# Decode attention plus SwiGLU on one core: the 38-row transfer of the output weights cut into 26 and 12 rows, and two strips of x moved from SyncE's DMA queue to GpSimd's

## The chip, the cores and the metric

The kernel runs on one core of a Trainium2 chip. A core has TensorE (PE; its weight loads are PEld), VectorE (DVE), ScalarE (ACT), GpSimd (POOL) and SyncE (SP), each with its own instruction queue, and 16 DMA engines. The metric is the device time of one execution in microseconds (us); lower is better. A profiled execution also gives a span, from the first to the last instruction of the core.

## The reference, cut to what matters

A transformer block for one new token in each of B = 4 sequences, with D = 640 channels, 32 heads of Dh = 192, and a window of W = 2048 cached positions; all in bf16.

```
xn  = layernorm(x)
q   = xn @ wq                                    # 640 x 6144
p   = softmax(q . k_cache[:, :, -2048:, :] * 192**-0.5)
o   = p . v_cache[:, :, -2048:, :]
a   = o @ wo                                     # 6144 x 640
f   = (silu(xn @ w1) * (xn @ w3)) @ w2           # 640 x 1536, 1536 x 640
out = x + a + f
```

Nearly all the bytes are read once: 201 MB of keys and values, 7.9 MB each of wq and wo, 3.9 MB of w1 and w3, 2.0 MB of w2.

## The kernel before, in words

**Layout.** A tile of keys or values holds 128 partitions (32 heads x 4 blocks of positions), each with 128 positions x 192 channels: 6144 KB, one transfer by `load` (issue at L109). The pool `kv` has three such buffers, so a load waits on SP until the tile that used its buffer three loads earlier has been read. A sequence needs four loads of keys and four of values.

**Keys** (`keys`): VectorE multiplies a quarter of the tile by the broadcast q (L211), TensorE adds 16-channel pieces by matmuls against an identity (L218), VectorE reduces the rest (L228). **Softmax** (`chain`): maximum, exponent (L251), row sums (`rowsum`). **Values** (`values`): VectorE spreads the probabilities over the heads (z, L267), and 64 matmuls (L279) multiply them by the tile; `evict` (L287) and `sort` (L295, L297) bring the result of a sequence into `oT`, the left operand of the output projection.

**Order.** The lists `units` and `stream` write out the order by hand: loads run ahead of their use by two. The last entries of `stream` are `gates` (w1 and w3 into one kv buffer, L320), `last_values` (the last tile of values as two halves, VS = 2, and then WI = 10 of the NI = 48 rows of the output weights that each partition holds, into a buffer of the pool `pr`), and `last_weights` (the other 38 rows of the output weights into a kv buffer, L304, and then w2 in three pieces of 8, 3 and 1 rows, L325). All of these are issued from SP, one behind another, on one DMA queue (q1 in the profile). `dve` and `pe` pin the order of the instructions of VectorE and TensorE to that of the program.

**End of the kernel.** `ffn_mm` (L332) and `ffn_transpose` (L348) make the gated hidden vector while the last values come in. Then the two halves of the last values, `evict`, `sort`, and `proj` (L311): for each of the 48 rows of the output weights two matmuls of 320 columns, first the 10 rows, then the 38 rows (76 matmuls). `acc` collects them. VectorE copies `acc` (L411) and adds `x_st` (L412). TensorE runs 24 matmuls of w2 (L419, two for each of its 12 rows), VectorE adds both (L422), and SP and ACT store half of the output each (L424, L425).

**The strips of x.** `x_st` holds x once more, cut in two strips of 320 columns at partitions 0 to 3 and 32 to 35, so that it has the layout of `acc`. GpSimd clears the tile (L120). `x_load` fills it by two DMAs of 2.5 KB from SP (L124); it is called in the main loop when the keys of sequence 2 begin.

Of the kernel before, what the change touches and what calls it, by code (L numbers as in the profile page):

```python
# [18 lines left out]
def kernel(  # L19
# [13 lines left out]
    CH: int = 32,  # L33
    R: int = 4,
    WI: int = 10,
    ALIGN: int = 64,
):

# [6 lines left out]
    nc = tc.nc  # L45
    P = 128
    B, Sq, D = A_x.shape
    _, H, Sk, Dh = A_k_cache.shape
# [3 lines left out]
    NJ = P  # L52
# [5 lines left out]
    NI = Dh // R  # L58
# [4 lines left out]
    DH = D // 2  # L63
# [12 lines left out]
    kvpool = ctx.enter_context(tc.tile_pool(name="kv", bufs=3))  # L76
    ppool = ctx.enter_context(tc.tile_pool(name="pr", bufs=2))
# [25 lines left out]
    def load(which, b, s, n0=0, n1=NJ):  # L103
        if n0 == 0:
            kv = kvpool.tile([P, NJ, Dh], BF16, tag="kv")
            kvs[which, b, s] = kv
        p0 = Sk - W + s * NJ * R
        rows = {"k": A_k_cache, "v": A_v_cache}[which][b, :, p0:p0 + NJ * R, :].rearrange("h (r n) d -> h r n d", r=R)
        nc.sync.dma_start(out=kvs[which, b, s][:, n0:n1, :].rearrange("p n d -> p (n d)"),  # L109
                          in_=rows[:, :, n0:n1, :].rearrange("h r n d -> h r (n d)"))  # L110
# [6 lines left out]
    x_rows = A_x.rearrange("b s d -> (b s) d")  # L117
    nc.scalar.dma_start(out=x_bf[:, 0, :], in_=x_rows)
    x_st = const.tile([64, DH], BF16, name="x_st")
    nc.gpsimd.memset(x_st[:], 0.0)  # L120

    def x_load():
        for t in range(2):
            nc.sync.dma_start(out=x_st[32 * t:32 * t + B, :], in_=x_rows[:, t * DH:(t + 1) * DH])  # L124

    wq_rows = A_wq.rearrange("(p kc) n -> p kc n", kc=KC)
    wq0 = kvpool.tile([P, NJ, Dh], BF16, tag="kv")
# [26 lines left out]
    at = (NH - 1) * NG * R  # L154
    for b in range(B):
        nc.vector.tensor_copy(out=qwin[:, b, at:at + NG * R].rearrange("p (g r) -> p g r", r=R),
                              in_=idf[:, b:P:32].unsqueeze(2).to_broadcast([P, NG, R]))
# [29 lines left out]
    for k in range(NH // 2):  # L187
        pool, tag = (ps_add, "ps") if k < 2 else (ps_o, "o_ps")
# [109 lines left out]

    wos, ffn = {}, {}

    def wo_load(i0, i1, pool, tag, shape):
        wt = pool.tile(shape, BF16, tag=tag)
        flat = wt[:].rearrange("p a n -> p (a n)")[:, 0:(i1 - i0) * D]
        nc.sync.dma_start(out=flat, in_=A_wo.rearrange("(p i) n -> p i n", i=NI)[:, i0:i1, :].rearrange("p i n -> p (i n)"))  # L304
        for i in range(i0, i1):
            wos[i] = flat[:, (i - i0) * D:(i - i0 + 1) * D]

    def proj(i0, i1):
        for i in range(i0, i1):
# [12 lines left out]
    def w2_load(i0, i1):  # L322
        if i0 == 0:
            ffn[2] = ffn["tile"][:, 2 * KC * F:2 * KC * F + NF * CF * D].rearrange("p (i n) -> p i n", n=D)
        nc.sync.dma_start(out=ffn[2][:, i0:i1, :], in_=B_w2.rearrange("(p i) n -> p i n", p=P)[:, i0:i1, :])  # L325
# [27 lines left out]
    def last_values():  # L353
        for g in range(VS):
            load("v", B - 1, NU - 1, g * NJ // VS, (g + 1) * NJ // VS)
        wo_load(NI - WI, NI, ppool, "pr", [P, WI, D])

    def gates():
        ffn_load(1)
        ffn_load(3)  # L360

    def last_weights():
        wo_load(0, NI - WI, kvpool, "kv", [P, NJ, Dh])
        for i0, i1 in ((0, (NF - 1) * CF), ((NF - 1) * CF, NF * CF - 1), (NF * CF - 1, NF * CF)):
            w2_load(i0, i1)

    units = [("k", 0, s) for s in range(NU)]
    for b in range(B):
        for s in range(NU):
            units += [("v", b, s)] + ([("k", b + 1, s)] if b < B - 1 else [])  # L370
    stream = [(load, u) for u in units[2:-1]] + [(gates, ()), (last_values, ()), (last_weights, ())]

    def feed():
# [4 lines left out]
    for which, b, s in units[:-1]:  # L378
        if which == "k":
            keys(b, s)  # L380
        else:
            if s == 0:
                reduces()
                chain(b)
            values(b, s)
        if stream:
            feed()
        if which == "k" and b > 0:
            reduces()
            if s == 0:  # L390
                rowsum(b - 1)
                if b == B // 2:
                    x_load()
            elif s == NU - 1:
                sort(b - 1)
        if which == "v" and s == NU - 1 and b < B - 1:
            evict(b)
        if which == "v" and s == 0 and b == B - 1:
            rowsum(b)
# [16 lines left out]
    for i in range(NF * CF):  # L416
        n, c = i // CF, i % CF
# [37 lines left out]
```

## Time and profile before

| | |
|---|---|
| three runs | 530.02, 530.15, 530.56 us; median 530.15 |
| the profiled execution | 529.3 us |
| its span | 527.4 us |
| read from HBM | 222.96 MB, 423 GB/s over the span |
| busy | PE 342.5 us, PEld 201.3, DVE 300.5, ACT 17.8, POOL 3.5 |
| mean granted clock of TensorE | 0.871 |

The span is what the views of the trace count from (0 is its first instruction). The times of the runs are longer than the span by what lies around it: 1.9 us in the profiled execution. "Idle before, releaser" behind a group says how long its engine had waited just ahead of it, and for whom. The chain of waits follows the last instruction back, at each step to what released it.

### The profile page before, as it was taken

The page shows a single profiled execution, that of the slowest core. Times are in us where ns is not written, and L with a number is a line of the kernel's source. Part 1 is how long each engine was busy: PE and PEld are TensorE (multiplying, and loading weights), DVE is VectorE, ACT ScalarE, POOL GpSimd, SP SyncE. Part 2 cuts the span into 40 slices and gives each one's busy share as a digit, 9 for nine tenths or more (in the row PEclk, how much of TensorE's full clock was granted, in tenths as well). Part 3 has the DMA queues.
Part 4 walks back from the last instruction along what each step waited for, and adds up shares of the span by engine and source line. Part 5 has one row for each costly group of instructions (what it writes and reads, how often), then busy time and mean ns, then how long its engine had stood idle before and what let it go on. Part 6 is the DMA issues. An engine that isn't in the chain of part 4 may idle for free.

```text
span 527.4 us, 4688 instructions
## 1 busy us (share of the span) xinstructions
PE 342.5 (65%) x2147; PEld 201.3 (38%) x2147; DVE 300.5 (57%) x189; ACT 17.8 (3%) x34; POOL 3.5 (1%) x11
## 2 busy tenths in 40 slices
PE   0517676676775876686566857686655758667646
PEld 0312332252534352354324342454323243555634
DVE  4018999768474839585584739494675748331100
ACT  2110000000000000000000000000000000002000
POOL 2000000000000000000000000000000000000000
PEclk9968999979898788798797888898897989798678
DMA  8999999999999999999999999999999999999992
GB/s 358 444 445 421 432 452 422 421 434 451 419 421 460 429 425 434 444 422 425 444 438 421 432 452 425 426 436 441 421 429 449 429 422 440 445 401 441 435 427 120
DMA packets 6108, 223.27 MB, mean 423 GB/s; under 512 B 692, under 2 KB 840, under 8 KB 968
## 3 DMA queue, kind: packets, MB, share of 16 engines
q1 hardware_dynamic: 6072, 222.96, 98.0%
q8 instruction: 17, 0.28, 0.2%
q14 instruction: 3, 0.02, 0.0%
q10 hardware_dynamic: 16, 0.01, 0.0%
HBM read 222.96 MB, written 0.01 MB: 423 GB/s over the span
## 4 chain that ended last, share of the span: by engine, by line
DMA 50%; DVE 27%; PE 21%; issue 1%; ACT 0%; SPq 0%; DVEq 0%; ACTq 0%
DMA kv<-in_A_k_cache_dram 38%; DVE pr L211 20%; PE o_ps L279 9%; PE ps L218 9%; DMA wt<-in_A_wo_dram 7%; DMA kv<-in_A_v_cache_dram 5%; DVE sc L228 4%; DVE z L267 3%; PE acc L311 1%; PE fp L295 1%; ACT e L251 0%; PE ft L419 0%; PE mt L246 0%; DVE gmax L243 0%; DVE lmax L239 0%
## 5 line engine op out<-in xcount | busy, mean ns | idle before, releaser
L211 DVE TENSOR_TENSOR pr<-kv,qb 128x6144 bf16<-128x6144 bf16 x64 | 213.4, 3351 | 106.1 <-DMA kv<-in_A_k_cache_dram 106.1
L218 PE MATMUL ps<-pr,idb 128*128 128x512 bf16 x768 | 194.1, 410 | 97.0 <-DVE pr L211 97.0
L218 PEld LDWEIGHTS <-idb 128*128 128x128 bf16 x768 | 79.2, 103 | 209.1 <-issue 124.4
L279 PE MATMUL o_ps<-kv,z 128*64 128x384 bf16 x1024 | 114.5, 396 | 51.8 <-DVE z L267 43.0
L279 PEld LDWEIGHTS <-z 128*64 128x64 bf16 x1024 | 96.4, 198 | 69.3 <-DVE z L267 52.7
L228 DVE TENSOR_REDUCE sc<-ps 128x32 f32<-128x512 f32 x64 | 44.0, 687 | 45.8 <-PE ps L218 45.8
L267 DVE TENSOR_TENSOR z<-e,selz 128x4096 bf16<-128x4096 bf16 (+1 forms) x17 | 36.7, 2158 | 16.9 <-PE o_ps L279 13.2
L411 DVE CAST t<-acc 64x320 bf16<-64x320 f32 x1 | 0.5, 482 | 26.0 <-PE acc L311 26.0
L311 PE MATMUL acc<-wt,oT 128*32 128x320 bf16 x96 | 9.6, 374 | 8.2 <-DMA wt<-in_A_wo_dram 7.6
L287 ACT COPY o_ev<-o_ps 128x384 f32<-128x384 f32 x4 | 1.9, 478 | 296.6 <-PE o_ps L279 296.6
L195 PE MATMUL qp<-wq,xnT 128*32 128x384 bf16 x80 | 6.3, 506 | 8.1 <-DMA wq<-in_A_wq_dram 8.1
L311 PEld LDWEIGHTS <-oT 128*32 128x32 bf16 x96 | 6.5, 118 | 11.2 <-issue 8.7
L295 PEld LDWEIGHTS fp<-o_ev,esel 128*128 128x128 f32 x64 | 7.7, 192 | 1.3 <-ACT o_ev L287 0.9
L295 PE MATMUL fp<-o_ev,esel 128*128 128x48 f32 x64 | 7.6, 273 | 0.6 <-ACT o_ev L287 0.6
L195 PEld LDWEIGHTS <-xnT 128*32 128x32 bf16 x80 | 3.5, 143 | 10.6 <-issue 7.7
L340 DVE TENSOR_TENSOR t_bf<-sg,t_bf 96x512 bf16<-96x512 bf16 x1 | 0.4, 421 | 11.6 <-ACT t_bf L334 11.6
L179 PE MATMUL xnT_ps<-idb,scratch 4*128 4x4 bf16 x5 | 0.4, 179 | 9.9 <-DVE scratch L175 9.9
L251 ACT ACTIVATE e<-sc,negm 128x512 bf16<-128x512 f32 x4 | 2.9, 722 | 78.7 <-DVE negm L248 78.7
L258 DVE RECIPROCAL rcp<-tb 128x1 f32<-128x1 f32 x4 | 0.6, 160 | 8.6 <-PE tb L256 8.6
L179 PEld LDWEIGHTS <-scratch 4*128 4x128 bf16 x5 | 0.3, 125 | 9.9 <-DVE scratch L175 9.9
L297 ACT ACTIVATE oT<-fp,rcp 128x48 bf16<-128x48 f32 x4 | 1.9, 468 | 60.9 <-PE fp L295 60.9
L204 PE MATMUL bp<-scratch 128*128 128x192 bf16 x32 | 3.3, 246 | 0.2
(59 smaller groups left out, 46.8 us busy)
## 6 DMA issues: line engine op xcount, KB each, us to landing
kv<-in_A_k_cache_dram SPq DMA_DIRECT2D x16, 6144.0 KB, 27.9
kv<-in_A_v_cache_dram SPq DMA_DIRECT2D x15, 6144.0 KB, 27.7
wq<-in_A_wq_dram SPq DMA_DIRECT2D x1, 6144.0 KB, 17.6
kv<-in_A_v_cache_dram SPq DMA_DIRECT2D x2, 3072.0 KB, 25.4
wt<-in_A_wo_dram SPq DMA_DIRECT2D x1, 6080.0 KB, 34.6
ft<-in_B_w_dram SPq DMA_DIRECT2D x2, 1920.0 KB
wt<-in_A_wo_dram SPq DMA_DIRECT2D x1, 1600.0 KB
wq<-in_A_wq_dram SPq DMA_DIRECT2D x1, 1536.0 KB, 20.7
```

The lines of the kernel that those rows point to most:

```text
L195: pe(nc.tensor.matmul(q_pss[k][32 * g:32 * g + 32, 0:QW], lhsT=xnT[:, kc, :], rhs=wq[:, 2 * k:2 * k + 2, g, :], start=(kc == 0), stop=(kc ...
L204: pe(nc.tensor.matmul(bp[:], lhsT=qwin[:, b, w0:w0 + P], rhs=q_sb[:, k, :], start=(k == 0), stop=(k == NH - 1)))
L211: dve(nc.vector.tensor_tensor(out=pr[:], in0=kvs["k", b, s][:, c * CH:(c + 1) * CH, :], in1=qb[:, b, :].unsqueeze(1).to_broadcast([P, CH, ...
L218: pe(nc.tensor.matmul(ps[:], lhsT=idb[:], rhs=pr[:, :, kk * DD:(kk + 1) * DD], start=(kk == 0), stop=(kk == NK - 1)))
L228: dve(nc.vector.tensor_reduce(out=scs[b][:, at:at + CH], in_=ps[:], axis=AX.X, op=ALU.add))
L251: nc.scalar.activation(out=e[:], in_=sc[:], func=ACTF.Exp, bias=negm[:, 0:1], scale=SCALE, accum_out=rs[:])
L267: dve(nc.vector.tensor_tensor(out=z[:].rearrange("p h (a j) -> p h a j", j=ZB), in0=es[b][:, at:at + n].rearrange("p (a j) -> p a j", j=ZB ...
L279: pe(nc.tensor.matmul(o_pss[b][64 * t:64 * t + 64, 0:2 * Dh], lhsT=zf[:, a:a + (2 * H - 1) * half + 1:half], rhs=vt[:, n0 + a:n0 + a + hal ...
L287: nc.scalar.copy(out=o_ev[:].rearrange("p t d -> p (t d)"), in_=o_pss.pop(b)[:, 0:2 * Dh])
L295: pe(nc.tensor.matmul(fp[:], lhsT=esel[:, t, R - 1 - c:R - 1 - c + P], rhs=o_ev[:, t, c * NI:(c + 1) * NI], start=(c == 0 and t == 0), sto ...
L297: nc.scalar.mul(out=oT[:, :, b:b + 1].rearrange("p i o -> p (i o)"), in_=fp[:], mul=rcps.pop(b)[:, 0:1])
L311: pe(nc.tensor.matmul(acc[32 * t:32 * t + 32, :], lhsT=oT[:, i, :], rhs=wos[i][:, t * DH:(t + 1) * DH], start=(i == i0 and i0 == proj0), s ...
```

## The change

`wo_load` takes a list of cuts and issues one transfer for each piece, all into one tile; the 38 rows come as rows 0 to 25 (4160 KB) and rows 26 to 37 (1920 KB), in this order, both from SP. The 10 rows still come as one transfer. `x_load` issues its two DMAs from GpSimd. Its call stands where it stood, but GpSimd's queue has no other instruction of the kernel's body behind the memsets of the beginning, so that nothing in that queue is ahead of them but these. The matmuls and their order are the same.

```
+    WM: int = 26,
...
     def x_load():
         for t in range(2):
-            nc.sync.dma_start(out=x_st[32 * t:32 * t + B, :], in_=x_rows[:, t * DH:(t + 1) * DH])
+            nc.gpsimd.dma_start(out=x_st[32 * t:32 * t + B, :], in_=x_rows[:, t * DH:(t + 1) * DH])
...
-    def wo_load(i0, i1, pool, tag, shape):
+    def wo_load(cuts, pool, tag, shape):
         wt = pool.tile(shape, BF16, tag=tag)
-        flat = wt[:].rearrange("p a n -> p (a n)")[:, 0:(i1 - i0) * D]
-        nc.sync.dma_start(out=flat, in_=A_wo.rearrange("(p i) n -> p i n", i=NI)[:, i0:i1, :].rearrange("p i n -> p (i n)"))
-        for i in range(i0, i1):
-            wos[i] = flat[:, (i - i0) * D:(i - i0 + 1) * D]
+        flat = wt[:].rearrange("p a n -> p (a n)")
+        for i0, i1 in zip(cuts, cuts[1:]):
+            at = (i0 - cuts[0]) * D
+            nc.sync.dma_start(out=flat[:, at:at + (i1 - i0) * D],
+                              in_=A_wo.rearrange("(p i) n -> p i n", i=NI)[:, i0:i1, :].rearrange("p i n -> p (i n)"))
+            for i in range(i0, i1):
+                wos[i] = flat[:, at + (i - i0) * D:at + (i - i0 + 1) * D]
...
-        wo_load(NI - WI, NI, ppool, "pr", [P, WI, D])
+        wo_load((NI - WI, NI), ppool, "pr", [P, WI, D])
...
-        wo_load(0, NI - WI, kvpool, "kv", [P, NJ, Dh])
+        wo_load((0, WM, NI - WI), kvpool, "kv", [P, NJ, Dh])
```

## The prediction

> **What bounds the kernel now.** I read the page first: the DMA queues, then the end of the chain of waits.
>
> ```profile
> q1 hardware_dynamic: 6072, 222.96, 98.0%
> ```
>
> q1 is SP's queue; its packets fill 98.0% of what 16 engines have in the span. So the stream of transfers is the floor, and compute is worth time only where it trails the last byte. The chain in order of time, its end:
>
> ```profile
> 474.30 7.17 PE o_ps L279 x64
> 481.48 34.64 DMA wt<-in_A_wo_dram
> 516.12 0.04 issue
> 516.16 6.76 PE acc L311 x76
> 522.92 1.65 PE ft L419 x24
> 524.56 0.02 issue
> 524.59 0.48 DVE res L422
> ```
>
> The 38 rows land at 481.48 + 34.64 = 516.12. Only then do their 76 matmuls run, then the 24 of w2, then the last addition. This is 8.5 us of work, but is the stream already over? The timeline of the end, with SP's issues and the rows that carry my durations:
>
> ```profile
> 471.89 1.19 SPq L109 DMA_DIRECT2D kv<-in_A_v_cache_dram  x2
> ...
> 481.87 1.38 SPq L325 DMA_DIRECT2D ft<-in_B_w_dram  x3
> ...
> 490.69 5.02 PE L279 MATMUL o_ps<-kv,z 128*64 128x384 bf16 x32 [4.09 <-DMA kv<-in_A_v_cache_dram]
> ...
> 497.95 4.55 PE L279 MATMUL o_ps<-kv,z 128*64 128x384 bf16 x32 [2.25 <-DMA kv<-in_A_v_cache_dram]
> ...
> 505.71 2.85 PE L311 MATMUL acc<-wt,oT 128*32 128x320 bf16 x20 [0.65 <-ACT oT L297]
> 516.16 6.76 PE L311 MATMUL acc<-wt,oT 128*32 128x320 bf16 x76 [7.60 <-DMA wt<-in_A_wo_dram]
> ...
> 522.74 1.80 PE L419 MATMUL ft<-ft,hT 128*32 128x320 bf16 x24
> ```
>
> The two halves of the last values, issued together, release TensorE at 490.69 and 497.95. So two transfers into one tile land one behind the other, 7.26 us for 3.146 MB (433 GB/s), and the first half's matmuls wait for the first alone. At that rate the 10 and the 38 rows (7.864 MB) need 18.16 us and should land at 497.95 + 18.16 = 516.11; they do. Behind them come the pieces of w2. The answer for the tile ft gives this landing line (the smallest piece is not in it):
>
> ```profile
> DMA to landing us min/median/max: 37.3/37.6/38.0
> ```
>
> Issued at 481.87 and 0.46 later, the first two pieces land at 519.17 and 520.33 (their 1.311 and 0.492 MB at 433 GB/s after 516.12: 519.15 and 520.28). The third, 0.164 MB, adds 0.38: 520.71. The stages show it too:
>
> ```profile
> 510.00:512.00 2.00, 0.00 (x0) 0.00 (x0) 0.00 (x0) 0.00 (x0) 0.00 (x0) 1.00 0.97 419
> 519.00:520.00 1.00, 1.00 (x17) 0.80 (x14) 0.00 (x0) 0.00 (x0) 0.00 (x0) 0.95 0.37 141
> 521.00:522.00 1.00, 1.00 (x20) 0.82 (x16) 0.00 (x0) 0.00 (x0) 0.00 (x0) 1.00 0.00 0
> ```
>
> The last three columns are granted clock, DMA share and GB/s. From 510 to 512 TensorE has nothing while the DMA runs at 0.97; after 521 it is the reverse. Of the tail, some 3.5 us can go without one byte coming sooner.
>
> **The cut, step by step.**
>
> 1. *Landing of the first part.* 12 rows are 1.966 MB, 4.54 us at 433 GB/s: 26 rows land at 516.12 - 4.54 = 511.58.
>
> 2. *Price of one more boundary in the queue.* Three whole loads land between 430.80 and 474.26 (the chain's ends), 14.49 us each, so half of one is 7.24; the halves above took 7.26. That is 0.02 us, which I take. Upper end: from 514 to 515, where the 38 rows end and w2 begins, DMA share was 0.51, so 0.5 us. Lower end: nothing, as no byte goes away. The Trainium skill, "DMA: Bandwidth & Descriptors", section "Anatomy of one DMA", fits a transfer as 2.0 us fixed plus its bytes; it names that mostly the wait for the last write's receipt. This trace has it beside the stream, since the halves' 7.26 us has no room for 2 us. What it would give if it stood in the queue is a rival below.
>
> 3. *SP's queue.* One more issue, some 0.46 us (1.38 / 3) in front of w2's three. These went out 32 us before their bytes moved, so it is covered; without cover it would be 0.46. A semaphore comes round again: the waits of SP show its store waiting for the first half of v (7.4 us, to 490.67), eight transfers before it (ScalarE's store counted). With one more, the third piece of w2 is eight behind w3, which landed when TensorE went on at 483.45; it would be issued then, still 30 us early. What is behind it on SP is the store alone.
>
> 4. *TensorE.* The 24 matmuls at clock 1.0 took 1.80: 65 ns each and 0.30 for the last to end. The 20 at 505.71, at clock 0.5 (0.50 in the half microseconds 506.0 to 508.5), took 2.85: 134 ns each. In that view the clock changes near 502.0, 505.4, 508.9, 512.3 and 519.1, steps of 3.41 us or twice that, and goes up one step after work has filled a step, down one after a step of idling. With the same steps, 52 matmuls from 511.62 get 0.65 us at 1.0 (10), 3.41 us at 0.5 (25), and 17 at 1.0: done at 516.8. The second part has landed by 516.14, so its 24 follow with no wait, to about 518.7 with the last one's end. Copy and addition (L411, L412: 0.48 and 0.32) end at 519.5, beside TensorE.
>
> 5. *What is late next: w2.* 16 matmuls from 519.19 end at 520.2, before the second piece (520.35); 6 more end at 520.75; the third piece is there at 520.73. The last two, 0.07 + 0.30, end at 521.1 to 521.2. Before, the 24 ended at 522.74 + 1.80 = 524.54. **Gain 3.4 us.** The addition, the stores (525.09) and the end move along.
>
> **The strips.** Removed: two issues on SP at 241.37, 0.83 us together. SP's next instruction is a load at 253.44 that waits for a buffer, so this frees nothing; 0.83 is the other end. Removed from q1: eight rows of 640 bytes, 5 KB, 0.01 us at 433 GB/s. Added: two issues by GpSimd behind its last memset (2.72 + 1.37 = 4.09). The trace of before has no DMA of GpSimd. Nearest rows: ScalarE's issue of x at 0.73, 0.55 us, and SP's at 0.42. GpSimd has nothing more to do, and L412 needs x_st near 519, so even 100 us for an issue is hidden. On the 16 engines 5 KB at the beginning instead of the middle: between -0.1 and +0.1. The first chain (x, normalisation, q) has cover: TensorE waits 8.05 us for wq at 18.33. I take 0. Queued behind the two DMAs on GpSimd is nothing but the end.
>
> **Sum.** 3.4 off 529.3 (the profiled execution; span 527.4 to 524.0) is 525.9. The median of the runs stands 0.85 above that execution, so by it: 530.15 - 3.4 = **526.8**.
>
> **Rivals.**
>
> *The second part is waited for as well* (one wait for the whole tile; the cut doesn't do what it says). Then 516.16 stays and 530.15 + 0.02 = 530.2. The halves of v, released at 490.69 and 497.95, speak against it. 4%.
>
> *A fixed price of 2.0 us in the queue.* If a boundary costs even a part of what stands idle, w2 and the end move by it; 2.0 gives 528.8. The 0.02 us above speaks against it; the dip at 514 speaks for a quarter of it. 4%.
>
> *The clock stays at 0.5.* The cut makes work thinner, and thin work lowered the clock above. All 76 from 511.62 at 134 ns end at 521.8, the 24 of w2 at 525.2 instead of 524.54: 530.8, a loss. It decides only if the clock stays low beyond 519.5; the steps at 508.9 and 519.1 each followed 3 us of work, against it. With half of the 100 matmuls slow the end is still w2's. 5%.
>
> *GpSimd's DMAs cost before the start (slower).* SP's first issue at 0.73 stands behind a barrier that GpSimd takes part in. If issuing DMAs from GpSimd makes it set something up ahead of that barrier, the whole stream moves by it. Nearest record: a drain of 2.74 us on GpSimd after two instructions that configure it, at 1.42. One for each of the two issues is 5.5: 526.8 + 5.5 = 532.3. It decides from 3.4 us. Against it: those records lie behind the barrier and delay nothing in the trace of before. The Trainium skill, "GPSIMD Engine Reference", section 2.1, has about 6 us for the first call of freshly loaded code; no row here shows it, and with 6 in place of 5.5 the rival would end at 532.8. 5%.
>
> **Chances and range.** The forecast 80%; the rivals 18%; 2% for other things. Its own range: down 0.83 (SP's issues were worth something) to 526.0, up 0.5 (boundary), 0.46 (issue), 0.1 and the spread of the runs (0.4) to 528.2. Taking in the fixed price, 526.0 to 528.9 holds 84%. Runs here tell about 0.2% (1.06 us) from no change: faster means below 529.1. Forecast, fixed price and half of the other things: faster 86% with a little of the clock's; same 8% (clock, whole wait); slower 6%.
>
> **What would show it.** Right: the 52 matmuls of L311 begin near 511.6, the other 24 end before 519.2, L419 comes in three groups that wait for the DMA of ft, and the chain ends with ft in place of wt at near 520.7, with span 524.0. SP shows three issues of the output weights; POOL's queue shows two near 4.1. Wrong: L311 begins at 516.1 (whole wait); w2 lands after 521.5 (price of the boundary); L419 is continuous and L311 ends after 520 (clock); SP's first issue is later than 0.73 or wq lands after 18.3 (GpSimd).

## The result, and the profile after

The changed kernel took 526.15 us (median of four runs, 525.88 to 526.65) against 530.2 before (530.02 to 530.56): ratio 0.9924, 95% interval 0.9907 to 0.9941, so 4.05 us or 0.76% faster, between 0.59% and 0.93%. Its profiled execution took 526.01 us with a span of 524.1. Lines of kernel.py stand four further down than before from `proj` on: L315 is the matmul of the output weights, L423 that of w2, L307 and L329 the issues of these weights. In the experiments below that add matmuls, later lines stand further down still (w2's matmul is L429 in most of them).

The queues, from its page:

```profile
q1 hardware_dynamic: 6200, 222.96, 98.6%
...
q0 software_dynamic: 64, 0.01, 0.0%
```

The same bytes on SP's queue, in 128 packets more (144 more for the cut, 16 fewer without the strips), and a small new queue, GpSimd's. The end of the chain of waits:

```profile
482.04 29.37 DMA wt<-in_A_wo_dram
511.41 0.04 issue
511.45 7.95 PE acc L315 x76
519.40 1.64 PE ft L423 x24
521.07 0.48 DVE res L426
```

The first part lands at 511.41 (511.58 was predicted), and the matmuls of the output weights start 4.7 us sooner than before. They run through in one piece. The 24 of w2 then begin with no wait, although the prediction had them waiting; the chain still has wt in it. From the timeline and from the view of the DMAs:

```profile
482.92 1.37 SPq L329 DMA_DIRECT2D ft<-in_B_w_dram  x3
...
519.23 1.80 PE L423 MATMUL ft<-ft,hT 128*32 128x320 bf16 x24
```

```profile
ft<-in_B_w_dram SPq DMA_DIRECT2D x1, 160.0 KB, 36.8
```

The third piece of w2, issued at 482.92 + 2 x 0.46 = 483.84, lands 36.8 later, at 520.64. The last two matmuls end at 519.23 + 1.80 = 521.03. Two matmuls after 520.64 need 0.04 + 0.37, also 521.05. So in this execution TensorE's row and w2 came out together, to within 0.1 us. The view by half microseconds (third column from the right: the granted clock) says why TensorE was as late as that:

```profile
509.50:510.00 0.50, 0.00 (x0) 0.00 (x0) 0.00 (x0) 0.00 (x0) 0.00 (x0) 0.99 1.19 512
510.00:510.50 0.50, 0.00 (x0) 0.00 (x0) 0.00 (x0) 0.00 (x0) 0.00 (x0) 0.50 0.57 246
...
516.50:517.00 0.50, 0.50 (x8) 0.38 (x6) 0.00 (x0) 0.00 (x0) 0.00 (x0) 0.69 0.86 353
517.00:517.50 0.50, 0.50 (x12) 0.39 (x10) 0.00 (x0) 0.00 (x0) 0.00 (x0) 1.00 0.69 287
```

The clock fell to 0.5 at 510.0, after TensorE had idled from 505.4, and came back only at 516.8, two steps of 3.41 us later. The prediction had one such step behind the landing.

### The profile page after: what moved, and what is told of

Read it like the earlier page. It is cut to its first block, busy times and chain, and to the rows that moved or that the text cites. A ratio compares the mean times of both kernels' runs of the same rounds, so it can differ in the third digit from the quotient of the medians.

```text
span 524.1 us, 4690 instructions
## 1 busy us (share of the span) xinstructions
PE 341.9 (65%) x2147; PEld 199.4 (38%) x2147; DVE 300.5 (57%) x189; ACT 17.8 (3%) x34; POOL 4.7 (1%) x13
## 4 chain that ended last, share of the span: by engine, by line
DMA 43%; DVE 29%; PE 25%; issue 1%; ACT 1%; SPq 0%; DVEq 0%; ACTq 0%
DMA kv<-in_A_k_cache_dram 38%; DVE pr L212 21%; PE o_ps L280 12%; PE ps L219 9%; DMA wt<-in_A_wo_dram 6%; DVE z L268 4%; DVE sc L229 4%; PE acc L315 2%; PE fp L296 1%; ACT e L252 1%; PE ft L423 0%; PE mt L247 0%; DVE gmax L244 0%; DVE gmq L246 0%; PE mt L242 0%
## 5 line engine op out<-in xcount | busy, mean ns | idle before, releaser
L280 PEld LDWEIGHTS <-z 128*64 128x64 bf16 x1024 | 94.5, 197 | 70.6 <-DVE z L268 53.0
L315 PE MATMUL acc<-wt,oT 128*32 128x320 bf16 x96 | 9.5, 371 | 6.7 <-DMA wt<-in_A_wo_dram 6.1
L196 PE MATMUL qp<-wq,xnT 128*32 128x384 bf16 x80 | 5.2, 440 | 7.9 <-DMA wq<-in_A_wq_dram 7.9
L315 PEld LDWEIGHTS <-oT 128*32 128x32 bf16 x96 | 6.5, 118 | 9.5 <-issue 7.0
```

Source lines behind the costliest of these rows:

```text
L196: pe(nc.tensor.matmul(q_pss[k][32 * g:32 * g + 32, 0:QW], lhsT=xnT[:, kc, :], rhs=wq[:, 2 * k:2 * k + 2, g, :], start=(kc == 0), stop=(kc ...
L280: pe(nc.tensor.matmul(o_pss[b][64 * t:64 * t + 64, 0:2 * Dh], lhsT=zf[:, a:a + (2 * H - 1) * half + 1:half], rhs=vt[:, n0 + a:n0 + a + hal ...
L315: pe(nc.tensor.matmul(acc[32 * t:32 * t + 32, :], lhsT=oT[:, i, :], rhs=wos[i][:, t * DH:(t + 1) * DH], start=(i == i0 and i0 == proj0), s ...
```

## The experiments

The theory on record before these runs, A: the last bytes of w2 set the end; whatever work stands behind the output weights' landing can be moved ahead of it, and nothing beyond that is to be had. B, the rival: TensorE's row from the landing on sets it, at the clock that it is granted. Others: the strips, and a price of a transfer of its own. Kernels that ran together share their runs of the kernel before, and each ratio is against these. Spans are given because each run has one, and they leave out what lies around it (1.7 to 2.1 us in nearly all).

**e0: the changed kernel once more.**

> The changed kernel as it is, to have its time and its clock steps once more beside the kernels of the same call. Theory A (the last bytes of w2 set the end: they land near 520.6 in the span, two matmuls and the addition follow): span 524.0 to 524.3, 0.63% to 0.68% off the time of before. Theory B (the end is that of TensorE's row of 76 and 24 matmuls, and the granted clock in the steps after the first part lands decides): the span varies with the place of the clock's steps, 524.1 where two slow steps follow the landing, up to 1 us more where they come later; where only one slow step follows, L423 waits for ft and the span is the same 524.0.

Measured: 525.98 us, ratio 0.9929 (0.9917 to 0.9941). Chain and timeline of its profiled execution:

```profile
482.47 36.78 DMA ft<-in_B_w_dram
519.25 0.04 issue
519.29 1.97 PE ft L423 x24
```

```profile
511.72 7.01 PE L315 MATMUL acc<-wt,oT 128*32 128x320 bf16 x76 [3.08 <-DMA wt<-in_A_wo_dram]
519.29 1.96 PE L423 MATMUL ft<-ft,hT 128*32 128x320 bf16 x24 [0.56 <-DMA ft<-in_B_w_dram]
```

The same program, and now the chain ends with ft: one step at 0.5 (512.4 to 515.8), 76 matmuls in 7.01 instead of 7.95, and TensorE waits 0.56 us for w2. The end of L423 is 521.25 here and 521.03 there. TensorE waits for w2 a second time, which the row above hides: behind 16 matmuls the 17th begins at 520.53, with w2's second piece, and the last eight run through. Five spans lie between 523.9 and 524.2, median 524.1. The spans of the 17 runs of the kernel before beside them spread from 527.1 to 528.7, median 528.2. So w2 holds the changed kernel in this execution, TensorE's row ends level with it in the other, and the changed kernel hardly feels the clock, where before feels it.

**e1, e2: the two parts of the change alone.**

```
# e1: the strips from SP in the middle, the cut as in the changed kernel
-            nc.gpsimd.dma_start(out=x_st[...], ...)
+            nc.sync.dma_start(out=x_st[...], ...)
# e2: the strips from GpSimd, one transfer of 38 rows
-        wo_load((0, WM, NI - WI), kvpool, "kv", [P, NJ, Dh])
+        wo_load((0, NI - WI), kvpool, "kv", [P, NJ, Dh])
```

> The cut alone; the strips come from SP in the middle, as before. If the strips are worth nothing: the time of the changed kernel within 0.1 us, span 524.1 to 524.3. The trace of after had the last packets of w2 0.14 us sooner than before; if that came from the strips, w2 lands 0.14 us later here. If the cut is not the cause of the gain: 530.2.

> The strips alone; the 38 rows come as one transfer. If the strips are worth nothing: 530.1, span 527.2 to 527.5, TensorE released by the output weights at 516.0 to 516.2. The part of the measured gain (4.05 us by the medians, 3.3 by the two profiled executions) that goes beyond the predicted 3.4 would be here if it came from SP's or the DMA queue's relief: then 529.5.

Measured: e1 525.68 us, ratio 0.9925 (0.9913 to 0.9937), as e0's 0.9929 (0.9917 to 0.9941). e2 530.31, ratio 1.0006 (0.9996 to 1.0015). The spans are 523.7 to 524.2 and 527.5 to 529.0. The cut is the whole gain; the strips are worth nothing that can be told, and if anything cost up to 0.15%. The last packet of w2 ends at 520.59 in e1 and at 520.57 in e0, so that its earlier end in after (520.30) did not come from the strips. e1's profiled execution is like that of after: its 76 matmuls take 7.98 us, and TensorE's row, not w2, ends the chain, with L423 done at 521.37. The timeline of after shows GpSimd's issues where the prediction put them:

```profile
4.06 1.19 POOL L125 DMA_DIRECT2D x_st<-in_A_x_dram  x2
```

**e9: the cut without its use.** The second part's rows are multiplied first, so that all 76 matmuls wait for the second landing.

```
-    proj(0, NI - WI)
+    proj(WM, NI - WI)
+    proj(0, WM)
```

> The cut stays, but TensorE takes the second part's 12 rows before the first part's 26, so that all 76 matmuls wait for the second landing. Theory A (the gain is the work that the first landing lets begin): as before, 76 matmuls from 516.2 and the 24 behind them, span 527.3 to 528.4 by the place of the clock's steps. If the gain came from two transfers in place of one: 524.1.

Measured: 529.85 us, ratio 1.0005 (0.9996 to 1.0014). The timeline of e2, where the 38 rows come as one transfer, and then that of e9:

```profile
516.24 7.44 PE L315 MATMUL acc<-wt,oT 128*32 128x320 bf16 x76 [10.59 <-DMA wt<-in_A_wo_dram]
```

```profile
516.21 8.09 PE L315 MATMUL acc<-wt,oT 128*32 128x320 bf16 x76 [9.00 <-DMA wt<-in_A_wo_dram]
```

Two transfers instead of one, and no gain: what counts is that work may begin at the first landing. The second part lands within 0.05 us of where the whole lands in before and in e2. The 76 took 8.09 us here, 6.76 in the profiled execution of before and 7.44 in that of e2, which start within 0.1 us of each other. They differ by how long the clock stays at 0.5 behind the landing: up to 519.1 in before, 520.6 in e2 and 521.9 in e9. Their spans are 527.4, 528.3 and 528.9. That is the spread of the kernel before.

**e4: before, with a busy clock.** Unused matmuls fill TensorE's idle time ahead of the 38 rows (their results go nowhere).

```
     proj(NI - WI, NI)
+    warm(30)      # 30 matmuls of 128x512 against the identity
     proj(0, NI - WI)
```

> The kernel before (one transfer of 38 rows, strips from SP) with 30 of the same unused matmuls between the 10 and the 38 rows, which keep TensorE busy from 508.6 to about 515. If the slow clock after the landing cost 1.5 us of the tail of before: 76 matmuls at 65 ns take 5.2 us in place of 6.8, span 525.9, so that clock alone explains a good 1.5 of the 3.4 us. If the gain of the cut is only in starting sooner and clock doesn't count: span 527.4.

Measured: 527.78 us, ratio 0.997 (0.9958 to 0.9982).

```profile
516.23 5.34 PE L311 MATMUL acc<-wt,oT 128*32 128x320 bf16 x76
```

5.34 us at clock 1.0, 1.4 less than in the profiled execution of before. The busy clock alone is worth 0.3% here, 2.2 us by the medians; seven of ten spans are 525.9 to 526.1, as expected, the others 527.5 to 527.7, and no trace of those is kept. The cut reaches further, because it lets about half of the 76 matmuls run ahead of the second landing, where e4 only makes them faster behind it.

**e5, e6: a late cut, without and with a busy clock.**

```
-    WM: int = 26,
+    WM: int = 34,
# e6 also: warm(36) between the 10 rows and the others
```

> The cut at row 34 in place of 26: the first part lands near 514.5, 68 matmuls follow. Theory A (only w2's landing sets the end, any cut that brings some work ahead is as good): span 524.1. Theory B (TensorE's row from the landing on, at the clock it is granted): 3.4 to 6.8 us of it at 134 ns, the rest at 65, end of L423 at 522.9 to 524.6, span 525.8 to 527.5; it depends on the place of the clock's steps.

> The cut at row 34 with 36 unused matmuls ahead of the 34 rows. If the clock is what the late cut loses by: the 76 matmuls at 65 ns end near 519.5, w2 sets the end again, span 524.1. If the late landing by itself is what it loses by: as the late cut without them, 525.8 or more.

Measured: e5 528.61 us, ratio 0.9975 (0.9966 to 0.9985); e6 527.12, ratio 0.9949 (0.9933 to 0.9964). First e5, then e6:

```profile
514.53 7.62 PE L315 MATMUL acc<-wt,oT 128*32 128x320 bf16 x76 [6.02 <-DMA wt<-in_A_wo_dram]
```

```profile
514.69 5.34 PE L315 MATMUL acc<-wt,oT 128*32 128x320 bf16 x76 [1.21 <-DMA wt<-in_A_wo_dram]
```

With the landing 3 us later, B holds: e5's row of 76 and 24 ends at 523.8, long after w2, and the busy clock takes 2.3 us off the 76. In e6 they end at 520.0, 0.5 us later than I expected, and the 24 of w2 follow at once to 521.7: still TensorE's row, at full clock, 0.5 us past the changed kernel. This is the quickest of e6's six executions: the spans go from 524.6 to 526.7, and what made the others longer is not shown. So w2's landing is the floor, and a cut reaches it only when the first part lands early enough: with two steps at half clock the 100 matmuls took 9.6 us in after (511.4 to 521.0). Row 26 just allows that; in e5 and e6 row 34 didn't.

**e7: ten pieces.** What does a boundary cost?

```
-        wo_load((0, WM, NI - WI), kvpool, "kv", [P, NJ, Dh])
+        wo_load(tuple(range(0, NI - WI, 4)) + (NI - WI,), kvpool, "kv", [P, NJ, Dh])
```

> The 38 rows as ten transfers of 4 rows (the last of 2): eight boundaries more than in the changed kernel, all else the same. At 0.02 us each: w2 lands 0.2 us later, span 524.3 (TensorE no longer idles long, so the matmuls are earlier than w2). At 0.5 each, the dip of the DMA share at 514 to 515 in the trace of before: 4 us, span 528. At the 2.0 us of the fixed price: 16 us, span 540. SP issues seven more transfers; if their waits for semaphores that come round let the queue run dry, the DMA share would fall between 490 and 514.

Measured: 527.85 us, ratio 0.9956 (0.994 to 0.9971); profiled span 525.9.

```profile
515.66 1.34 PE L315 MATMUL acc<-wt,oT 128*32 128x320 bf16 x12 [0.82 <-DMA wt<-in_A_wo_dram]
519.46 3.39 PE L423 MATMUL ft<-ft,hT 128*32 128x320 bf16 x24 [2.47 <-DMA ft<-in_B_w_dram]
```

w2's first piece releases TensorE at 519.46. The same wait ended at 519.29 in e0 and between 519.12 and 519.21 in e3, e8 and e11 below, so eight boundaries cost 0.2 to 0.3 us, 0.02 to 0.04 each. That is about the term of the prediction; the fixed price of 2 us would have put the release near 535. SP's queue did not run dry: w2 is issued only at 506.3 here (482.9 in after), but the DMA share is 1.0 from 509.8 to 516.6. But the kernel is slower than the changed one, by a way that I had not expected here: the pieces feed TensorE 8 matmuls (0.72 us) every 1.5 us, the clock goes to 0.5 at 516.6, TensorE then has nothing to do for 2.47 us, and the 24 of w2 take 3.39 instead of 1.96. It is the prediction's rival of the clock, in a kernel that is cut too finely.

**e3, e8, e10, e11: can the changed kernel be bettered by a busy clock, and what stands in the way?** e3 puts 20 unused bf16 matmuls into TensorE's idle time, e8 seven fp32 ones (the trace has 14 matmuls for these, and 19 for e3's). e10 and e11 put 16 and 3 matmuls of four columns near 488, where nothing waits for them.

```
     proj(NI - WI, NI)
+    warm(20)      # e3: 128x512 bf16; e8: warm(7), 128x384 fp32
     proj(0, NI - WI)
...
     ffn_transpose()
+    tiny(16)      # e10; e11: tiny(3)
```

> The changed kernel with 20 matmuls (128 x 512 against the identity, result unused) between the 10 rows and the 26 rows, 4.3 us at full clock where TensorE had been idle for 6.1 us. Theory A: the 76 matmuls run at clock 1.0 and end near 517.9, L423 waits for the third piece of w2, the end is the same within 0.1 us (span 524.0). Theory B alone, without a floor by w2: end 1.2 us sooner, span 522.9. If the extra matmuls fall into a slow step they end late, and the 26 rows start late: up to 525.5.

> The changed kernel with 7 unused fp32 matmuls of 384 columns in TensorE's idle stretch, in place of 20 in bf16: about the same 4.5 us of work in fewer instructions. In the run with 20, one 16 KB transfer of the instruction queue began at 519.68, between the last packets of w2, and w2 landed 1.2 us later than in the changed kernel. If that was it, here (fewer instructions, so TensorE comes later to that place) w2 lands near 520.8 again, TensorE waits for it at full clock, span 524.0 to 524.3. If the extra matmuls slow the stream by themselves: 525.6 again.

> The changed kernel with 16 unused matmuls of 4 columns in TensorE's idle stretch before the last values (near 488), some 1 us of work that nothing waits for, but 32 more instructions ahead of the end. Theory C (a 16 KB transfer of the instruction queue is set off when TensorE comes to a certain place in its program; here it is set off some 16 matmuls earlier, at 519.6 in place of 520.7, and delays the last packets of w2): span 525.2 to 526.1, w2 landing near 521.8. If the late landing in the runs with extra matmuls came from their work or the full clock: 524.1, as the changed kernel.

> The same with 3 tiny matmuls, 6 instructions. Theory C: the instruction transfer comes some 3 matmuls earlier than in the changed kernel, at 520.5, where the last packets of w2 are over or nearly so: span 524.1 to 524.3. If any additional matmul there delays the end: more than 524.5.

Measured: e3 527.24 us (ratio 0.9954, 0.9941 to 0.9966), e8 526.92 (0.9941, 0.9927 to 0.9954), e10 526.16 (0.9928, 0.9915 to 0.994), e11 526.48 (0.9935, 0.9921 to 0.9949). None is better than the changed kernel, and e3 is over 1 us slower. e11's spans, 523.9 to 524.4, are those of the changed kernel; its longer median lies outside the span (up to 3.1 us in its runs). The timeline of e3 and two of its half microseconds:

```profile
519.12 1.26 PE L429 MATMUL ft<-ft,hT 128*32 128x320 bf16 x16 [1.24 <-DMA ft<-in_B_w_dram]
521.84 0.72 PE L429 MATMUL ft<-ft,hT 128*32 128x320 bf16 x8 [1.46 <-DMA ft<-in_B_w_dram]
```

```profile
520.00:520.50 0.50, 0.38 (x6) 0.14 (x3) 0.00 (x0) 0.00 (x0) 0.00 (x0) 1.00 0.01 3
520.50:521.00 0.50, 0.00 (x0) 0.00 (x0) 0.00 (x0) 0.00 (x0) 0.00 (x0) 1.00 0.05 8
```

Here the waits that the prediction expected can be seen, though two and not three: TensorE, at full clock and done early, waits for w2 ahead of 16 matmuls and ahead of the other 8. But w2 is late: from 520 to 521 nearly nothing moves (DMA share 0.01 and 0.05, of 16 engines), and the last packets end at 521.8 instead of 520.3 to 520.6. In the packet records a 16 KB packet of the instruction queue (q8) fills 519.68 to 520.64. The last packet of w2 ahead of the gap ends at 520.07, and the last ten run one behind another from 520.62 on. In e8's profiled execution it is the same (519.62 to 520.59, w2's last packet at 521.9).

I took that as the cause: TensorE, being earlier, reaches the place that sets off this transfer before w2 is through. The further tests do not settle it. e8 was meant to move the packet behind w2; it came at 519.62 all the same, and its spans run from 524.2 to 526.1. e10 was meant to bring it on with no change of the clock. The packet came at 519.93, and w2 ended at 520.3 undisturbed; one of its five spans is 525.2, the others 524.1 to 524.5. e11 was meant to bring it on to 520.5; it came at 522.2, after w2. In e6 a packet at 519.93 did no harm either, nor did one in e4 at 519.73, 0.05 us later than e3's. So the two coincide in e3 and e8, but a packet at that time is not enough. The ten packets in a row would fit one DMA engine that had part of w2 still to move when it took the 16 KB, and no harm where the engine that took it was through. The records don't name the DMA engine of a packet, so that this is not shown, and the cause stays open.

## Why the prediction was right, point by point

- **What bounds the kernel** (the stream; only the tail is to be had): right. Where TensorE is early (e0), it waits for w2; where it is late (after), its end and what w2's landing allows stand within 0.1 us of each other. No variant went below a profiled span of 524.1, and the shortest of all spans is 523.7 (e1).
- **Step 1, landing of the first part**: 511.58 predicted, 511.41 in after, 511.68 in e0.
- **Step 2, the boundary at 0.02 us**: e7 gives 0.02 to 0.04 for each of eight more. TensorE is released by the last of the 38 rows at 516.21 in e9, with the boundary, and at 516.24 in e2 and 516.16 in before, without it. The rival of 2 us falls. The Trainium skill, "DMA: Bandwidth & Descriptors", section "Anatomy of one DMA", which the prediction cites there, gives its fit for DMAs issued by GpSimd; these transfers are SP's.
- **Step 3, SP's queue**: covered, as predicted. The waits of SP in after show the store waiting for the second half of the values, 13.4 us, where before it was the first half.
- **Step 4, TensorE**: the mechanism held (the first part's matmuls run beside the second part's transfer, no wait between them), and the size was off in the profiled execution. One step at 0.5 behind the landing was assumed, and all 76 done by 518.7. It had 5.4 us at 0.5, and they were done at 519.4. e0 has one, and its 76 end at 518.73. The steps lie differently in each execution; I had carried over the place of those of one. The forecast stood that, since w2 sets the end as long as no more than about half of the 100 matmuls are slow, as the prediction's rival of the clock says (40 were, by 5.4 us at 134 ns). Its reading that the clock goes "down one after a step of idling" was too simple. In before it fell at 505.4 although TensorE had been busy for 2.46 us of that step, and in e7 at 516.6 after 1.66 us. Nor does any work bring it back: at half clock 2.85 and 2.93 us of work in a step did (before, at 508.9 and 519.1), 1.95 us in after (by 513.4) and 2.35 us in e10 (by 513.8) did not. Where the limit lies is not shown.
- **Step 5, w2 late next**: end of L423 predicted at 521.1 to 521.2; 521.03 in after and 521.25 in e0. ft in the chain showed in e0 and e3, not in after, where the extra step at 0.5 used up the slack to the last 0.1 us. The three groups were two: in e0 the second piece came 0.2 us later than the 520.35 of the prediction, at 520.53, and the third was there before its matmuls' turn.
- **The strips at nothing**: right (e1 and e2). The rival of a cost before the start falls: SP's first issue is at 0.74 in after (0.73 before), and e2 is not slower by more than 0.15%.
- **The sum**: span 524.0 predicted, 524.1 measured. The time was put at 526.8 and came out at 526.15 and 525.98. The mis-sized term is the last one, "the median of the runs stands 0.85 above that execution". I took it as something around the span that stays. It isn't: the time outside the span was 1.83 us before and 1.91 after (means of e0's runs and of those of before beside them). The spans of before spread over 1.6 us, and the profiled execution with its 76 matmuls in 6.76 us was one of the quick ones (527.4, median 528.2). The change takes that spread away with the work that was exposed to the clock. From median to median the gain in spans is 528.2 - 524.1 = 4.1, of which 3.4 were predicted. The other 0.7 fit the clock's cost in a median execution of before beyond that of the profiled one: e2's profiled execution, with a span of 528.3, has its 76 matmuls in 7.44 us, 0.68 more. The range held by little, and not for the reason given: its lower end, 526.0, stood for SP's issues, which were worth nothing, and e0's 525.98 and e1's 525.68 lie just below it.
- **The rival of the clock** came up where the work was fed late (e5) or thinly (e7), and cost 2.3 us (e5's 76 matmuls against e6's) and 1.4 us (e7's 24 against e0's) there. In the changed kernel's profiled executions the clock was back at 1.0 by 516.8, far from the 519.5 from which the prediction had it decide.

## What to carry to other kernels

When the stream of transfers is full to the end, the only time to gain is the work behind the last landings. Cut the last large transfer so that most of that work can begin earlier, and check that it starts early enough to be through by the next transfer's landing with as much half clock as the executions show (here two steps); cutting finer costs little in the queue, but in e7 it fed TensorE too thinly to keep its clock. A median that stands above the profiled execution is a spread to be explained (here from the clock's steps), not a constant to be added.

## What the runs showed of the hardware that was not expected

- The place of the clock's steps of 3.41 us changes from execution to execution of the same program: half clock from 510.0 to 516.8 in one profile of the changed kernel, from 512.4 to 515.8 in the other. The same 76 matmuls took 6.76, 7.44 and 8.09 us behind the same landing in three executions (before, e2, e9). The Trainium skill, "TensorE: Matmul & The Clock Gate", Part 1, has the window of activity as free-running, not reset when a kernel starts; the profiles agree, and the prediction should have drawn from it that one profile's steps are one draw.
- Two DMAs of 2.5 KB issued by GpSimd made 64 packets on their queue (8 of them data; SP's two before made 16 in all), 0.6 us each to issue and 7.8 and 10.8 us to land, at a time when the 16 engines were full (DMA share 1.0 or more from 4 to 16 us).
- A 16 KB packet of the instruction queue took 0.96 us near the end of e3, and w2's next packet began as it ended; in e4, e6 and e10 one of the same size at about the same time held up nothing.
